# A Fourier filter and a low-rank mixer: new residue order in the last stage, one pair of batch 0 copied straight to its rows, free rows cleared by two engines

## The chip, the cores and the metric

The kernel runs on one core of a Trainium2 chip. A core has five engines with their own instruction queues: PE (TensorE, matrix products; PEld is its weight load), DVE (VectorE), ACT (ScalarE), POOL (GpSimd) and SP (SyncE, which here only issues transfers). Transfers issued by SP and by POOL share sixteen transfer engines. The metric is the device time in microseconds; the kernel before took 522.15 us (median of three runs, 521.4 to 522.26).

## The reference

Shapes: x is 8 batches x 3136 positions x 256 channels; U is 3136 x 32, V is 32 x 3136, w1 is 256 x 1024, w2 is 1024 x 256.

```python
X = np.fft.rfft(x, axis=1)
y = np.fft.irfft(X * (filt_r + 1j * filt_i)[None], n=3136, axis=1)
u = y + (y.transpose(0, 2, 1) @ U @ V).transpose(0, 2, 1)
out = u + np.maximum(u @ w_ch1, 0.0) @ w_ch2
```

Each batch is filtered along the positions, a rank-32 mixture of the positions is added, and a two-layer network runs on the channels of every position.

## The kernel before

A position is written as 64 q + r, with q below 49 and r, the residue, below 64. A transform of length 3136 becomes a 49-point step over q and a 64-point step over r, each a matrix product. Of the 49 frequencies k1 of the first step only 0 to 24 are needed.

For a batch b the stages are:

- **f1 (L203 to L246)**: the 49-point transform of x. For batches 0 and 1 it leaves the data in SBUF (`f1_turned`), and `turn` (L248) transposes it; the others pass through DRAM.
- **mid (L271)**: for each pair of k1 (twelve pairs, and k1 = 0 alone) a 64-point transform (L325), the product with the filter on DVE (L333), and the transform back (`s3`, L286; product L292, copy to `e3` on ACT L302). `gm` and `gsm` are its matrices; their 64 output rows per real or imaginary part are the 64 residues r.
- **rank (L364)**: the product with the transformed U (`uh`, made once by `u_hat`, L181), which gives 32 rows `h1`; four DVE copies (L383) spread them over all residues.
- **s4 (L390)**, the last stage of the filter: for each residue r the 97 rows `eb[:, r, :]` are multiplied with `sv[:, r, :]`. Rows 0 to 31 of `eb` are the mixer's, row 96 is k1 = 0, and of rows 32 to 95 every fourth, with offset 0, 1 or 2, holds eight k1 values (real and imaginary) of part 0, 1 or 2. Rows with offset 3 carry nothing: `sv` is zero there, but `eb` must hold numbers. s4 handles eight residues at a time, in two halves: the even groups of eight first, then the odd ones (`g = 2 * (n % 4) + n // 4`).
- **mm1, mm2 (L427, L448)**: the two layers, on groups of 512 positions, the residual added by products with an identity (L446).

`e3` has residues on partitions, `eb` needs k1 on partitions. That turn goes through DRAM: `s3` stores four k1 at a time (L307) into `ct2[b][part]`, and `load_e2` (L353) loads a part back with two transfers, one for the even groups (h = 0) and one for the odd (h = 1). In batch 0 the last two pairs (21, 22 and 23, 24) are each stored on their own (L304). `fill` (L359) copies 512 KB of some constant into the offset-3 rows of `eb` once.

The order of the work is written out by hand. Ahead of the steady state stand `u_hat`, f1 and mid of batch 0, its loads, its rank stage, half of batch 1's f1 mixed with 13 matmuls on constants (`pw`, L513) that keep PE busy, and s4 of batch 0. POOL's copy `seen` (L515), which reads a few numbers of `eb`, holds back the x and w2 transfers behind it until `eb` is loaded. From there one loop runs mm1 and mm2 over the 49 groups, with the stages of the next batches dealt into it by a list `plan`.

The lines that the change and the prediction's steps touch: the filter copies `spread_filters` (L152, called at L317), `s3` (L291, L303), `load_e2` and `fill` with their calls (L494 to L504), `rank` (L368, L383), `s4` (L399) and `pw` (L510). SP issues in this order in batch 0: two stores of part 0 with k1 = 0's row between them, `fill`, two stores of part 1, two loads of part 0, the store of pairs 8 and 9 (counted from 0), those of pairs 10 and 11, two loads of part 1, two of part 2. A queue works in order: an instruction that waits holds all behind it.

Of the kernel before, what the change touches and what calls it, by code (L numbers as in the profile page):

```python
# [10 lines left out]
F16 = mybir.dt.float16  # L11
F32 = mybir.dt.float32
# [9 lines left out]
GT = 512  # L22
NG = NB * SEQ // GT


# [5 lines left out]
def _consts():  # L31
# [25 lines left out]
    rows = [64 * c + 32 * h + j for j in range(32) for c in range(2) for h in range(2)]  # L57
    m64 = np.concatenate([a2[rows], g, gs, 2 * a2], axis=1)

# [14 lines left out]
def kernel(  # L74
# [58 lines left out]
    for c in range(4):  # L133
        load_x(0, c)
    m64 = cst.tile([128, 512], F16)
    nc.sync.dma_start(m64, m64_d)
    a2m, gm, gsm = m64[:, 0:128], m64[:, 128:256], m64[:, 256:384]
    a20m = m64[0:64, 384:512]


# [30 lines left out]
    sv = cst.tile([97, NR, NQ], F16)  # L171

    seen = cst.tile([128, 4], F16)

# [3 lines left out]

    uh = cst.tile([128, NK, RANK], F16)

    def u_hat():  # L181
        tu = sb.tile([RANK, 24, 128], F16, tag="ut", bufs=2, name="tu")
        tu0 = sb.tile([RANK, NR], F16, tag="tu0", bufs=1, name="tu0")
        for n in range(8):
            pu = bank("zmzo"[n % 4], "puh")
            for i in range(4):
                j = 4 * n + i
                nc.tensor.matmul(pu[0:RANK, 98 * i:98 * i + 98], usb[:, j, :], ws[:, j * 98:j * 98 + 98],
                                 start=(i == 0), stop=True, skip_group_check=True)
            copy = nc.vector.tensor_copy if n % 2 else nc.scalar.copy  # L190
            copy(tu.rearrange("p k (c j) -> p k c j", c=4)[:, :, :, 4 * n:4 * n + 4],
                 view(pu[0:RANK], 0, [[1, 24], [24, 4], [98, 4]]))
            copy(view(tu0, 4 * n, [[1, 4], [32, 2]]), view(pu[0:RANK], 96, [[98, 4], [1, 2]]))
        pt = bank("z", "put", F16)
        for k in range(NK):
            src = tu[:, k - 1, :] if k else tu0
            m = 128 if k else NR
            nc.tensor.transpose(pt[0:m, RANK * k:RANK * k + RANK], src, idn[0:RANK, 0:RANK])
        nc.vector.tensor_copy(uh[:, 1:NK, :].rearrange("r k u -> r (k u)"), pt[:, RANK:RANK * NK])
        nc.vector.tensor_copy(uh[0:NR, 0, :], pt[0:NR, 0:RANK])  # L200
# [70 lines left out]
    def mid(b, tag="z"):  # L271
# [14 lines left out]
        def s3(ks, uv, o):  # L286
# [3 lines left out]
            pe = bank(tag, "pe")  # L290
            for f, w in enumerate((gm, gsm) if b == 0 else (gm,)):  # L291
                nc.tensor.matmul(pe[0:m, 0:n], w[:, 0:m], uv[:, f, o:o + n], start=(f == 0), stop=(b > 0 or f == 1))  # L292
# [9 lines left out]
            nc.scalar.copy(t[:, 2 * (i % 2):2 * (i % 2) + 2, :].rearrange("p k d -> p (k d)"), pe)  # L302
            if b == 0 and i > 9:  # L303
                nc.sync.dma_start(dram(ct2[b][2], 2 * (i % 4) * 128 * DM, [[DM, 128], [128 * DM, 2], [1, DM]]),  # L304
# [10 lines left out]
        for i, ks in enumerate(PAIRS[:first_at] + [(0,)] + PAIRS[first_at:]):  # L315
            n = len(ks) * DM
            if b == 0 and i == 2:  # L317
                spread_filters(1)
# [29 lines left out]

    def blocks(rows, h):

        return rows.rearrange("p (q h r) d -> p h q r d", h=2, r=8)[:, h]

    def load_e2(b, part):  # L353

        for h in range(2):
            nc.sync.dma_start(blocks(eb[32 + part:96:4], h).rearrange("p q r d -> p q (r d)"),
                              dram(ct2[b][part], 8 * h * DM, [[NR * DM, 16], [16 * DM, 4], [1, 8 * DM]]))

    def fill():  # L359

        nc.sync.dma_start(eb[35:96:4].rearrange("p (q r) d -> p q (r d)", r=8),
                          dram(ws_d.tensor, 0, [[8 * DM, 16], [16 * 8 * DM, 8], [1, 8 * DM]]))

    def rank(b):  # L364
        ph = bank("z", "ph")
        for i in range(24):
            c = i % 4
            nc.tensor.matmul(ph[32 * c:32 * c + 32, 0:DM], uh[:, i + 1, :], e3[b, i // 4][:, i % 4, :],  # L368
                             start=(i < 4), stop=(i >= 20 and c != 0))
# [20 lines left out]
    def s4(b):  # L390
        ut[b] = sb.tile([128, 2, NQ, NR], F16, tag="ut", bufs=2, name="ut")
        for n in range(8):
            g = 2 * (n % 4) + n // 4
            for dh in range(2):
# [3 lines left out]
                for i in range(8):  # L398
                    nc.tensor.matmul(pu[:, NQ * i:NQ * i + NQ], eb[:, 8 * g + i, d], sv[:, 8 * g + i, :],  # L399
                                            start=(i == 0), stop=True, skip_group_check=True)  # L400
# [180 lines left out]
```

## Time and profile before

| | |
|---|---|
| median of three runs | 522.15 us (521.4 to 522.26) |
| the profiled execution | 521.98 us, span 520.2 us |
| PE busy | 497.6 us, 96% of the span |
| DVE, ACT, POOL busy | 347.3, 372.9, 80.7 us |
| bytes moved by transfers | 88.79 MB, mean 171 GB/s |
| first matmul of all (U's transform, L188) | 7.34 us |
| first matmul of s4, batch 0 (L399) | 45.44 us |
| first matmul of the two layers (L431) | 50.25 us |

Times of single instructions are counted from the start of the span. "Landing" of a transfer is the moment at which its completion is marked; a transfer has sixteen such marks, and the last one releases who waits. A row of the windows view gives a stretch, its length, and for PE, PEld, DVE, ACT and POOL the busy time with the number of instructions, then the granted clock of PE, the share of the transfer engines and GB/s.

### The profile page before, as it was taken

The numbers are of one execution on the slowest core, as the hardware profiler recorded it, in microseconds if no ns is written. First come the engines' busy times: TensorE is split into PE (matmuls) and PEld (weight loads), VectorE is DVE, ScalarE is ACT, GpSimd is POOL, SyncE is SP. The second block draws the span as 40 slices with busy tenths as digits, with TensorE's granted clock in tenths as the row PEclk, the third lists the DMA queues.
The fourth block names the chain that finished last, engine by engine and source line by source line (L and its number), as shares of the span: only waits on it lengthen the run. The fifth ranks groups of instructions, "written<-read, shape, count | busy, mean of one in ns | idle before, by whom it ended". The sixth has DMA issues, their size and how long they took to land.

```text
span 520.2 us, 11846 instructions
## 1 busy us (share of the span) xinstructions
PE 497.6 (96%) x4807; PEld 352.5 (68%) x4807; DVE 347.3 (67%) x465; ACT 372.9 (72%) x704; POOL 80.7 (16%) x111
## 2 busy tenths in 40 slices
PE   3787999999999999999999999999999999999996
PEld 3535666776667767777667767776777766776665
DVE  2976698688847975788747975789656995631212
ACT  3765779767985789667985689667975777666662
POOL 5862010111010120011010120111010010101110
PEclk9998999999999999999999999999999999999999
DMA  8997846758686596818776596819785145212213
GB/s 190 175 277 177 140 105 201 232 192 166 186 259 212 101 221 206 291 66 180 189 243 229 104 221 207 289 67 195 212 237 195 62 146 185 99 42 81 82 49 114
DMA packets 67605, 88.79 MB, mean 171 GB/s; under 512 B 4811, under 2 KB 51979, under 8 KB 67552
## 3 DMA queue, kind: packets, MB, share of 16 engines
q0 software_dynamic: 14640, 41.52, 32.7%
q1 hardware_dynamic: 52912, 46.53, 29.1%
q8 instruction: 37, 0.61, 0.5%
q14 instruction: 16, 0.13, 0.1%
HBM read 55.79 MB, written 47.91 MB: 199 GB/s over the span
## 4 chain that ended last, share of the span: by engine, by line
PE 88%; DMA 4%; DVE 3%; POOL 2%; ACT 1%; issue 1%; SPq 0%; ACTq 0%; POOLq 0%
PE pc L454 32%; PE phh L431 32%; PE pu L399 5%; PE pf L212 4%; PE pc L446 4%; PE pe L292 4%; PE pz L325 3%; DVE uv L333 2%; DMA x<-in_x_dram 2%; PE ph L368 1%; DMA fab<-in_filt_r_dram 1%; POOL fab L157 1%; DMA ct<-e 1%; POOL x L121 1%; DMA eb<-ct 1%
## 5 line engine op out<-in xcount | busy, mean ns | idle before, releaser
L434 ACT ACTIVATE h<-phh 128x512 f16<-128x512 f32 x392 | 236.2, 604 | 88.8 <-PE phh L431 87.7
L431 PE MATMUL phh<-ut,w1sb 128*128 128x512 f16 (+7 forms) x896 | 234.7, 354 | 0.5 <-DVE ut L406 0.3
L454 PE MATMUL pc<-w2sb,h 128*128 128x256 f16 x1568 | 234.1, 272 | 0.0
L454 PEld LDWEIGHTS <-h 128*128 128x128 f16 x1568 | 151.5, 97 | 90.4
L461 DVE COPY och<-pc 128x512 f32<-128x512 f32 x98 | 67.6, 690 | 101.1 <-PE pc L446 99.5
L333 DVE TENSOR_TENSOR uv<-pz,fab 128x1024 f16<-128x1024 f32 (+1 forms) x104 | 120.9, 1180 | 13.3 <-PE pz L325 11.9
L466 POOL DMA_DIRECT2D out_dram<-och x48 | 39.1, 815 | 407.2 <-DVE och L461 391.4
L431 PEld LDWEIGHTS <-w1sb 128*128 128x128 f16 x896 | 77.7, 98 | 20.4 <-issue 2.4
L302 ACT CAST e<-pe 128x512 f16<-128x512 f32 x96 | 56.6, 591 | 20.8 <-PE pe L292 20.5
L406 DVE CAST ut<-pu 128x392 f16<-128x392 f32 x92 | 48.5, 559 | 20.9 <-PE pu L399 17.7
L217 ACT CAST asb<-pf 98x512 f16<-98x512 f32 x96 | 57.3, 599 | 0.2
L446 PE MATMUL pc<-idn,ut 128*128 128x128 f16 (+1 forms) x400 | 54.0, 219 | 0.0
L383 DVE COPY eb<-h 32x4096 f16<-32x4096 f16 x32 | 38.2, 1232 | 16.1 <-ACT h L380 16.0
L292 PE MATMUL pe<-uv,m 128*128 128x512 f16 (+1 forms) x117 | 41.6, 373 | 3.5 <-DVE uv L333 2.2
L399 PE MATMUL pu<-sv,eb 97*128 97x49 f16 x1024 | 39.3, 187 | 3.3 <-DMA eb<-ct 3.3
L446 PEld LDWEIGHTS <-ut 128*128 128x128 f16 (+1 forms) x400 | 38.1, 98 | 5.2 <-issue 0.8
L399 PEld LDWEIGHTS <-eb 97*128 97x128 f16 x1024 | 36.4, 98 | 4.5 <-issue 3.7
L325 PE MATMUL pz<-a,m 128*128 128x512 f16 x96 | 36.2, 379 | 1.4 <-DVE a L263 1.2
L212 PE MATMUL pf<-x,ws 98*98 98x256 f16 x192 | 36.8, 274 | 0.0
L337 DVE TENSOR_TENSOR uv<-uv 64x1024 f16<-64x1024 f16 (+1 forms) x49 | 30.9, 630 | 1.7
L338 DVE TENSOR_TENSOR uv<-uv 64x1024 f16<-64x1024 f16 (+1 forms) x49 | 30.7, 627 | 0.7
L212 PEld LDWEIGHTS <-ws 98*98 98x98 f16 x192 | 22.0, 125 | 9.0
(61 smaller groups left out, 200.3 us busy)
## 6 DMA issues: line engine op xcount, KB each, us to landing
out_dram<-och POOLq DMA_DIRECT2D x48, 512.0 KB, 3.9
eb<-ct SPq DMA_DIRECT2D x48, 256.0 KB
ct<-e SPq DMA_DIRECT2D x47, 256.0 KB
x<-in_x_dram POOLq DMA_DIRECT2D x28, 392.0 KB, 8.0
ct<-asb SPq DMA_DIRECT2D x24, 384.0 KB
a<-ct SPq DMA_DIRECT2D x18, 512.0 KB
x<-in_x_dram POOLq DMA_DIRECT2D x4, 384.0 KB, 8.0
ws<-ws SPq DMA_DIRECT2D x1, 600.2 KB
```

The source lines that it names most:

```text
L212: nc.tensor.matmul(pf[0:98, 256 * s:256 * s + 256], ws[:, (8 * c + j) * 98:(8 * c + j + 1) * 98], t[:, j, :], start=(s == 0), stop=True, s ...
L217: nc.scalar.copy(dst, src)
L292: nc.tensor.matmul(pe[0:m, 0:n], w[:, 0:m], uv[:, f, o:o + n], start=(f == 0), stop=(b > 0 or f == 1))
L302: nc.scalar.copy(t[:, 2 * (i % 2):2 * (i % 2) + 2, :].rearrange("p k d -> p (k d)"), pe)
L325: nc.tensor.matmul(pz, a2m, src[:, k:k + 2, :].rearrange("p k d -> p (k d)"), start=True, stop=True)
L333: nc.vector.tensor_mul(uv[:, :, o:o + n], zin, fin)
L399: nc.tensor.matmul(pu[:, NQ * i:NQ * i + NQ], eb[:, 8 * g + i, d], sv[:, 8 * g + i, :], start=(i == 0), stop=True, skip_group_check=True)
L431: nc.tensor.matmul(ph[:, o:o + n], w1sb[:, dh, 128 * t:128 * t + 128], utv(b)[:, dh, t0:t0 + n], start=(dh == 0), stop=(dh == 1), skip_gro ...
L434: nc.scalar.activation(h, ph, RELU)
L446: nc.tensor.matmul(d, w, idn, start=False, stop=(dh == 1), skip_group_check=True)
L454: nc.tensor.matmul(o, gr.h[tt][:, 128 * i:128 * i + 128], w2sb[:, tt, :], start=(tt == 0), stop=False, skip_group_check=True)
L461: nc.vector.tensor_copy(gr.och[:, i - 1:i + 1, :], gr.pc.rearrange("p (j d) -> p j d", d=DM))
```

## The change

Five things are changed together.

1. **Residue order.** `eb` keeps its 64 residues as the 32 of the even groups followed by the 32 of the odd groups, instead of in natural order. `load_e2`, the four copies of `rank` and s4's reads of `eb` go to contiguous halves. Where rows reach `eb` without passing through DRAM, the transform back must give its residues in that order, so permuted copies of `gm` and `gsm` (`gmp`, `gsmp`) are added to the constant m64, which grows from 512 to 768 columns. They are used for k1 = 0 in all batches and for the last pair of batch 0. The matching U rows are permuted too: in `tu0`, and for the last pair in two extra entries of `uh`.
2. **The last pair of batch 0** (k1 = 23, 24) goes from `e3` straight into its four rows of `eb`, each row by one transfer of 64 pieces of 512 bytes, two on SP and two on POOL. The last load of part 2 then has 12 rows instead of 16 in that batch.
3. **Free rows.** `fill` is gone. At the very start DVE clears rows 0 to 95 of the first half of `eb`, and ACT clears those of the second half by copying a zero.
4. **Order on the queues.** Part 1's loads of batch 0 are issued one step earlier, ahead of pair 10's store; `spread_filters(1)` runs one step earlier.
5. **Filler.** 10 matmuls `pw` instead of 13.

```diff
+ORDER = np.concatenate([8 * (2 * (i % 4) + i // 4) + np.arange(8) for i in range(8)])
...
-    m64 = np.concatenate([a2[rows], g, gs, 2 * a2], axis=1)
+    p64 = np.concatenate([ORDER, 64 + ORDER])
+    m64 = np.concatenate([a2[rows], g, gs, 2 * a2, g[:, p64], gs[:, p64]], axis=1)
...
-    m64 = cst.tile([128, 512], F16)
+    m64 = cst.tile([128, 768], F16)
...
+    gmp, gsmp = m64[:, 512:640], m64[:, 640:768]
...
+    zero = cst.tile([128, 1], F32)
+    nc.vector.memset(zero, 0)
+    for h, rows in enumerate((eb[0:96, 0:32], eb[0:96, 32:64])):
+        rows = rows.rearrange("p r d -> p (r d)")
+        if h:
+            nc.scalar.copy(rows.bitcast(F32), bass.AP(tensor=zero.tensor, offset=zero.offset, ap=[[zero.ap[0][0], 96], [0, 4096]]))
+        else:
+            nc.vector.memset(rows.bitcast(mybir.dt.uint32), 0)
...
-    uh = cst.tile([128, NK, RANK], F16)
+    uh = cst.tile([128, NK + 2, RANK], F16)
...
-            copy(view(tu0, 4 * n, [[1, 4], [32, 2]]), view(pu[0:RANK], 96, [[98, 4], [1, 2]]))
+            copy(view(tu0, 32 * (n // 2 % 2) + 8 * (n // 4) + 4 * (n % 2), [[1, 4], [16, 2]]), view(pu[0:RANK], 96, [[98, 4], [1, 2]]))
...
+        tp = sb.tile([RANK, 2, 128], F16, tag="tp", bufs=1, name="tp")
+        nc.scalar.copy(view(tp, 0, [[64, 4], [32, 2], [8, 4], [1, 8]]), view(tu, 128 * 22, [[64, 4], [8, 2], [16, 4], [1, 8]]))
+        pd = bank("z", "pd", F16)
+        for k in range(2):
+            nc.tensor.transpose(pd[:, RANK * k:RANK * k + RANK], tp[:, k, :], idn[0:RANK, 0:RANK])
+        nc.scalar.copy(uh[:, NK:, :].rearrange("r k u -> r (k u)"), pd[:, 0:2 * RANK])
...
-            for f, w in enumerate((gm, gsm) if b == 0 else (gm,)):
+            direct = b == 0 and ks[0] == 23
+            ms = (gmp, gsmp) if direct or not ks[0] else (gm, gsm)
+            for f, w in enumerate(ms if b == 0 else ms[:1]):
...
-            if b == 0 and i > 9:
+            if direct:
+                for n, k in enumerate(ks):
+                    for part in range(2):
+                        (nc.sync if part else nc.gpsimd).dma_start(
+                            eb[32 + row_of(k, part):33 + row_of(k, part), :, :], t[64 * part:64 * part + 64, 2 + n, :])
+            elif b == 0 and i > 9:
...
-            if b == 0 and i == 2:
+            if b == 0 and i == 1:
                 spread_filters(1)
...
     def load_e2(b, part):
 
+        n = 12 if (b, part) == (0, 2) else 16
         for h in range(2):
-            nc.sync.dma_start(blocks(eb[32 + part:96:4], h).rearrange("p q r d -> p q (r d)"),
-                              dram(ct2[b][part], 8 * h * DM, [[NR * DM, 16], [16 * DM, 4], [1, 8 * DM]]))
-
-    def fill():
-
-        nc.sync.dma_start(eb[35:96:4].rearrange("p (q r) d -> p q (r d)", r=8),
-                          dram(ws_d.tensor, 0, [[8 * DM, 16], [16 * 8 * DM, 8], [1, 8 * DM]]))
+            nc.sync.dma_start(eb[32 + part:32 + 4 * n:4, 32 * h:32 * h + 32, :].rearrange("p (q r) d -> p q (r d)", r=8),
+                              dram(ct2[b][part], 8 * h * DM, [[NR * DM, n], [16 * DM, 4], [1, 8 * DM]]))
...
-            nc.tensor.matmul(ph[32 * c:32 * c + 32, 0:DM], uh[:, i + 1, :], e3[b, i // 4][:, i % 4, :],
+            nc.tensor.matmul(ph[32 * c:32 * c + 32, 0:DM], uh[:, i + (3 if b == 0 and i > 21 else 1), :], e3[b, i // 4][:, i % 4, :],
...
-            nc.vector.tensor_copy(blocks(eb[0:32], g // 2)[:, 2 * (g % 2):2 * (g % 2) + 2],
-                                  bass.AP(tensor=h1.tensor, offset=h1.offset, ap=[[h1.ap[0][0], 32], [0, 2], [0, 8], [1, DM]]))
+            nc.vector.tensor_copy(eb[0:32, 16 * g:16 * g + 16, :],
+                                  bass.AP(tensor=h1.tensor, offset=h1.offset, ap=[[h1.ap[0][0], 32], [0, 16], [1, DM]]))
...
-                    nc.tensor.matmul(pu[:, NQ * i:NQ * i + NQ], eb[:, 8 * g + i, d], sv[:, 8 * g + i, :],
+                    nc.tensor.matmul(pu[:, NQ * i:NQ * i + NQ], eb[:, 8 * n + i, d], sv[:, 8 * g + i, :],
...
-        if i == 7:
-            fill()
         if i == 10:
             load_e2(0, 0)
     next(ranks[0])
+    load_e2(0, 1)
     next(mids[0])
-    load_e2(0, 1)
...
-    for i in range(13):
+    for i in range(10):
...
-        nc.tensor.matmul(pw, m64[:, 0:128], m64, start=(i == 0), stop=(i == 12))
+        nc.tensor.matmul(pw, m64[:, 0:128], m64[:, 0:512], start=(i == 0), stop=(i == 9))
-    nc.gpsimd.tensor_copy(seen[64:96], eb[64:96, 8, 0:4])
+    nc.gpsimd.tensor_copy(seen[64:96], eb[64:96, 40, 0:4])
```

More of the change, by code (lines that the diff above doesn't have):

```diff
@@ L346, in mid @@
         yield
-    def blocks(rows, h):
-        return rows.rearrange("p (q h r) d -> p h q r d", h=2, r=8)[:, h]
     def load_e2(b, part):
+        n = 12 if (b, part) == (0, 2) else 16
         for h in range(2):
-            nc.sync.dma_start(blocks(eb[32 + part:96:4], h).rearrange("p q r d -> p q (r d)"),
-                              dram(ct2[b][part], 8 * h * DM, [[NR * DM, 16], [16 * DM, 4], [1, 8 * DM]]))
-    def fill():
-        nc.sync.dma_start(eb[35:96:4].rearrange("p (q r) d -> p q (r d)", r=8),
-                          dram(ws_d.tensor, 0, [[8 * DM, 16], [16 * 8 * DM, 8], [1, 8 * DM]]))
+            nc.sync.dma_start(eb[32 + part:32 + 4 * n:4, 32 * h:32 * h + 32, :].rearrange("p (q r) d -> p q (r d)", r=8),
+                              dram(ct2[b][part], 8 * h * DM, [[NR * DM, n], [16 * DM, 4], [1, 8 * DM]]))
     def rank(b):
```

## The prediction

> **What bounds the kernel now.** I read the page's busy shares first, then the chain of work that ended last, then the windows, waits and SP's timeline around the one stretch where TensorE stands still.
>
> The page's busy shares and the summary of its chain:
>
> ```profile
> PE 497.6 (96%) x4807; PEld 352.5 (68%) x4807; DVE 347.3 (67%) x465; ACT 372.9 (72%) x704; POOL 80.7 (16%) x111
> ...
> PE 88%; DMA 4%; DVE 3%; POOL 2%; ACT 1%; issue 1%; SPq 0%; ACTq 0%; POOLq 0%
> ```
>
> TensorE is the bound for nearly all of the span, and the change takes none of its steady work away. Whatever it is worth lies in the non-PE part of the chain, before batch 0's last stage ends. The chain in order of time (start us, length us, what):
>
> ```profile
> 36.03 0.60 ACT e L302
> 36.67 0.29 PE ph L368 x2
> ...
> 38.57 3.31 DMA ct<-e
> 41.95 0.52 SPq L356
> 42.52 2.94 DMA eb<-ct
> 45.46 4.15 PE pu L399 x120
> 49.63 0.58 DVE ut L406
> 50.25 3.58 PE phh L431 x8
> ```
>
> The last pair's output is ready at 36.62 and the last stage (L399) starts at 45.46: a store to DRAM, SP's turn, a load back. The stretches around it (busy time per engine, clock, transfer share, GB/s):
>
> ```profile
> 30.00:38.00 8.00, 6.00 (x46) 2.21 (x45) 5.35 (x5) 4.18 (x9) 4.07 (x1) 1.00 1.02 281
> 38.00:42.00 4.00, 4.00 (x43) 2.37 (x40) 3.67 (x4) 3.90 (x17) 0.00 (x0) 1.00 0.91 296
> 42.00:46.00 4.00, 0.74 (x23) 0.59 (x23) 1.06 (x2) 0.00 (x0) 0.00 (x0) 1.00 0.50 173
> 46.00:50.30 4.30, 3.98 (x114) 3.88 (x111) 4.00 (x8) 3.48 (x8) 3.26 (x6) 0.63 0.58 94
> ```
>
> Up to 42 the transfer engines are full (share 1.02, 0.91), and PE has filler; from 42.2 to 45.4 PE is idle. So the wait is a transfer backlog first and a latency second. SP's own timeline shows the order in that backlog:
>
> ```profile
> 27.44 0.37 SPq L307 DMA_DIRECT2D ct<-e  x1
> 27.86 0.61 SPq L361 DMA_DIRECT2D eb<-ws  x1
> 30.25 2.25 SPq L307 DMA_DIRECT2D ct<-e  x2
> 35.31 1.18 SPq L356 DMA_DIRECT2D eb<-ct  x2
> 36.54 1.43 SPq L307 DMA_DIRECT2D ct<-e  x1
> 38.07 0.97 SPq L304 DMA_DIRECT2D ct<-e  x2
> 39.20 3.91 SPq L356 DMA_DIRECT2D eb<-ct  x4
> ```
>
> The sixteen landing marks of each transfer (median, last) are, in SP's order: second store of part 0 34.76, 35.24; fill 36.01, 36.44; the two stores of part 1 36.78, 38.69 and about 37.5, 39.18; loads of part 0 38.48, 39.74 and 39.11, 40.35; pairs 8-9 40.18, 41.11; pair 10 40.62, 41.48; pair 11 40.99, 41.88; loads of part 1 41.93, 43.21 and 42.73, 43.83; loads of part 2 44.62, 45.35 and 45.39, 45.97. The last stage starts 0.09 us after the 45.35.
>
> **The change part by part.** The sum is against the profiled execution: 521.98 us, of which the span is 520.2; the median of the runs shown is 522.15, 0.17 above it.
>
> *Zeroing at the start.* DVE clears 4,096 words a partition. No row shows that instruction; the fp16 copy of 4,096 elements (L383) takes 1.23 us and the fp32 product of 1,024 elements (L333) 1.18 us, so 1.2 to 4.7 us; from 0.75 it ends by 5.5. ACT copies 4,096 words: L157 needed 1.90 us for 2,048, so 3.8 us, behind the table load that ends at 2.02, hence 5.8. DVE's first work before is at 8.21 and ACT's at 7.88, both behind U's landing (7.29). Cost 0; the cover is that landing. What could uncover it is a rival below.
>
> *m64 grows by half.* 64 KB more among the first loads. Below: 0, if it runs beside the wait for U. Above: 64 KB at the 177 GB/s of the first 8 us, 0.37 us. Its own median packet (64 ns for 1 KB) gives 128 x 32 ns / 16 = 0.26. U's load, which starts PE, runs beside it, so I take 0.15 and keep 0 to 0.37.
>
> *u_hat.* Two more transposes on PE: 25 took 0.95, so 0.08. Two ACT copies, 0.2 to 0.5 each (L193 0.18, L191 0.47): the first can start when DVE's last copy ends, 10.8, while PE is transposing until 11.84; the second is done about when ACT's next one began (12.39). I take 0.08, range 0 to 0.5.
>
> *spread_filters(1) one step earlier.* DVE's 0.76 us copy moves from 22.39 to about 21.1, ahead of a product; DVE's total is the same. It ran beside POOL's first filter copy, which took 3.01 us against 2.74 for the second. If that 0.27 goes, the product that waits for POOL at 28.47 can start when DVE is free, 28.31: -0.16, range -0.16 to 0.
>
> Together these three move the first stage by -0.16 to +0.87; I take +0.07.
>
> *The backlog: what goes.* The fill (median step 34.76 to 36.01 = 1.25 us of the queue), and pair 11's store (0.37).
>
> *What comes or moves.* Four one-row transfers (128 KB in 512 B pieces, as pair 11's store): 0.37 together, half on POOL's queue, half on SP behind pair 10's store. The two loads of part 1 are now issued before pair 10's store. They wait for part 1's second store; with the fill gone its median moves from 37.5 to 36.25, its last mark from 39.18 to 37.9, and behind that wait on SP stand pair 10's store, the two direct rows and the last load.
>
> *Why the 1.25 does not arrive whole.* Part 0's loads wait for the 35.24 landing, which lies ahead of the fill. Issue at 35.31 and 2.67 us (part 2's load, 41.95 to a median of 44.62) give a median landing of 37.98, against 38.48 now: only 0.50 of the 1.25. From there by median steps: second load 0.63 (38.61), pairs 8-9 1.07 (39.68), POOL's direct rows 0.19 (39.87), part 1's loads 0.63 to 0.80 each (41.13 to 41.47), pair 10 0.44: 41.57 to 41.91. The last of sixteen marks was 0.86 behind the median for pair 10 and 0.73 for a load that found the queue empty, 0.18 without its one laggard: so 41.75 to 42.77, against the 41.88 that releases SP now. SP by itself gives: wait ends 37.9, two loads at 0.6, store issued at 39.1, landing 2.3 later (the 2.29 of a store at 67.80 that met no queue): 41.4. Between 41.4 and 42.77 I take 41.9, nearest to the step sum without a full laggard: 0.0 against now.
>
> *The last load.* From issue to last mark 3.40 before, with other loads still ahead of it up to 43.83; now nothing but two small rows. Bounds: 2.85 (its marks without the laggard, 44.80) to 3.40; I take 3.1: -0.3. It has 12 rows instead of 16: by bytes 48 packets instead of 64, a quarter off about 0.64 (four packets of 159 ns an engine), -0.16. The Trainium skill (DMA: Bandwidth & Descriptors, "Why a DMA increments its semaphore by 16 and not by 1") says that a transfer is spread over the largest number of engines up to 16 that divides the outer size of both sides, hence 12 here, with four packets each as before; by that rule this saves nothing and the sum is the one without it. No run so far shows a transfer of 12 rows, and I take 0.
>
> *The direct rows themselves.* SP's are issued by about 40.4 and need 2.66 (the row at 69.87 landed at 72.53): 43.1. POOL is free from 34.07, waits for 36.62, issues two at about 0.55; even the slow 5.8 us of the early filter loads gives 43.5. Behind them POOL holds the copy `seen`, two x loads and w2sb, which wait for 45.97 anyway. Cost 0, covered by the last load; if that came before 43.5 they would be late next.
>
> *Filler.* Three of 13 matmuls less, 0.22 each: 0.65 less PE work ahead of an idle 3.2 us. Cost 0. The clock is at half from 47.1 to 53.9 already; the last stage does not feel it, since DVE's eight evictions of 0.54 fill 45.9 to 50.2.
>
> *Batches 1 to 7.* The same transfers, the same 32x4096 copies (1.2 us), other addresses; under PE's 96%: 0.
>
> *After the last stage.* `seen` releases x and w2sb; w2sb lands at 56.81 and the first matmul on it runs at 57.76. They move with the loads, so the start shift reaches the end.
>
> Sum: +0.07 + 0.0 - 0.3 = -0.23. 521.98 - 0.23 = 521.75; beside the median, 521.9. I forecast **521.8 us**. Ends: -0.16 - 0.48 - 0.55 = -1.19 and +0.87 + 0.89 + 0 = +1.76.
>
> **The rivals.** *Faster.* The relief is passed on: pair 10's store lands at SP's own 41.4 (-0.48) and the last load comes without a laggard (-0.55), -0.1 at the start: -1.13, 520.85, or 521.0 beside the median. For it: SP's queue would be short. Against: the step sum.
>
> *Slower: SP's queue.* One mark of part 1's second store is late again (its last is now 1.7 us behind its median) and comes at 39.18 as before. Then loads are issued at 39.20 and 39.88, pair 10's store at 40.5, landing at 42.8 to 43.9 (2.3, or the 3.4 of now): +0.9 to +2.0; middle 523.4. It decides once that store's wait ends after 38.4. Against: the fill's 1.25 us stand straight ahead of that store.
>
> *Slower: the start.* POOL's issue of U and x is held up by DVE's clearing, from 1.27 until 1.95 to 5.5; U, and everything behind it, comes 0.7 to 4.2 later: 522.7 to 526. Against: POOL's issues at 17.87 and 18.51 beside two DVE copies took 0.65 and 0.50, as ever. The Trainium skill (SBUF — State Buffer, "Who interferes with whom") says a DVE instruction with at most one SBUF input outside the two-port modes doesn't contend with GpSimd, which by its wording leaves a memset out; no run so far shows one.
>
> *Hidden anyway.* The last load's laggard stays: 0 to +0.07, 522.1.
>
> **How the numbers follow.** Forecast 0.38, hidden anyway 0.14, faster 0.25, SP's queue 0.15, start 0.08. About 0.2% (1.04 us) is what a measurement of this kernel can tell from no change. Faster: the 0.25 and 0.05 of the forecast's tail: 0.30. Slower: 0.15 + 0.08 - 0.02 = 0.21. Same: 0.49. The range takes in the faster rival's bound and SP's queue: 520.2 to 523.5; the forecast alone 521.0 to 522.6.
>
> **What would show it.** Right: no L361 row; part 0's loads issued within 0.3 us of 35.3; last landing of pair 10's store 41.5 to 42.3; L399's first matmul at 44.9 to 45.6; PE's idle stretch before it no shorter than 3 us. Wrong: that matmul before 44.4 or after 46.4, first U matmul after 7.8, or time found behind 58 us.

## The result and the profile after

The changed kernel takes 524.43 us (median of 7 runs, 523.38 to 526.17), against 522.15 us (7 runs, 520.52 to 523.13) for the kernel before beside it. The ratio is 1.0048, with a 95% interval of 1.0026 to 1.0069: the kernel got slower by about half a per cent, 2.3 us. The forecast was 521.8 us, in a range of 520.2 to 523.5. The profiled execution took 523.38 us with a span of 521.6 us, the shortest of its seven; the one before took 521.98 with 520.2. So the two traces differ by 1.40 us, less than the medians.

The busy shares and the summary of the chain of waits, from the page of the changed kernel:

```profile
PE 498.1 (95%) x4806; PEld 353.1 (68%) x4806; DVE 351.0 (67%) x467; ACT 377.0 (72%) x707; POOL 81.3 (16%) x113
...
PE 89%; DMA 4%; DVE 4%; ACT 1%; issue 1%; POOL 0%; DVEq 0%; SPq 0%; ACTq 0%; POOLq 0%
```

TensorE's work is the same to half a microsecond. The loss lies outside it, as the forecast had it of the gain. The chain of the changed kernel in order of time (start us, length us, what), from the last pair to the first matmul on w2sb:

```profile
36.31 0.59 ACT e L328
36.95 0.29 PE ph L391 x2
...
39.18 4.51 DMA ct<-e
43.69 0.02 issue
43.71 0.03 SPq L384
43.74 0.03 issue
43.77 3.12 DMA eb<-ct
46.88 0.30 issue
47.19 1.51 PE pu L422 x32
48.69 0.92 POOL x L127 x2
49.61 0.20 issue
49.81 9.55 DMA w2sb<-in_moe_w_ch_dram
59.36 0.04 issue
59.40 0.60 PE pc L477 x4
```

Before, the store in this place took from 38.57 to 41.88 and the last stage began at 45.44. Now it is pair 10's store, from 39.18 to 43.69, and the last stage begins at 47.19. The store's last mark is 1.81 us later, the last stage 1.75 us later. The delay runs on through the copy that releases x and w2sb: w2sb lands at 59.36 instead of 56.81, and the first matmul on it runs at 59.40 instead of 57.76, 1.64 us later. Before, that matmul ran 0.95 us behind the landing; now it runs 0.04 us behind it. What follows gives back 0.24 of that in this pair of traces (1.64 against the 1.40 of the profiled times).

The same stretches as before the change (busy time per engine, clock, transfer share, GB/s):

```profile
30.00:38.00 8.00, 5.93 (x41) 2.13 (x42) 5.63 (x5) 4.57 (x9) 5.11 (x3) 1.00 0.85 209
38.00:42.00 4.00, 3.82 (x43) 2.35 (x41) 3.39 (x3) 3.79 (x17) 0.27 (x1) 1.00 0.94 278
42.00:46.00 4.00, 0.00 (x0) 0.00 (x0) 1.23 (x2) 0.18 (x2) 0.00 (x0) 0.81 0.38 112
46.00:50.30 4.30, 3.11 (x76) 3.14 (x77) 2.08 (x4) 1.71 (x4) 1.79 (x4) 0.50 0.32 84
```

In the first row the transfer share fell from 1.02 to 0.85: the fill is gone, and its time was left empty; the loads behind it did not come earlier. In the third row PE does nothing at all for 4 us, and the clock falls within it. The last row shows the last stage at half the clock, with 76 matmuls in this stretch where there were 114.

SP's timeline of the changed kernel (start us, length of the issues us, what):

```profile
35.98 1.23 SPq L384 DMA_DIRECT2D eb<-ct  x2
37.32 0.52 SPq L338 DMA_DIRECT2D ct<-e  x1
37.95 1.18 SPq L384 DMA_DIRECT2D eb<-ct  x2
39.18 0.59 SPq L335 DMA_DIRECT2D ct<-e  x1
39.81 1.15 SPq L332 DMA_DIRECT2D eb<-e  x2
43.77 1.74 SPq L384 DMA_DIRECT2D eb<-ct  x2
```

Read from the top: part 0's loads, the store of pairs 8-9, part 1's loads, pair 10's store (39.18, before at 38.07), the two direct rows, and after a gap of almost 3 us the last load, which needs pair 10's store. The landing marks (median, last): part 0's loads 38.81, 39.10 and 39.73, 40.97; POOL's direct rows last at 41.06 and 41.84; pairs 8-9 40.89, 42.02; part 1's loads last at 42.66 and 43.33; pair 10 43.19, 43.69; SP's direct rows last at 44.14 and 44.33. Pair 10's store moved behind two loads of 256 KB, and landed behind them.

### The profile page after: what moved, and what is told of

It reads as the page before. It is cut to its first block, busy times and chain, and to the rows that moved or that the text cites. A ratio compares the mean times of both kernels' runs of the same rounds, so it can differ in the third digit from the quotient of the medians.

```text
span 521.6 us, 11857 instructions
## 1 busy us (share of the span) xinstructions
PE 498.1 (95%) x4806; PEld 353.1 (68%) x4806; DVE 351.0 (67%) x467; ACT 377.0 (72%) x707; POOL 81.3 (16%) x113
## 4 chain that ended last, share of the span: by engine, by line
PE 89%; DMA 4%; DVE 4%; ACT 1%; issue 1%; POOL 0%; DVEq 0%; SPq 0%; ACTq 0%; POOLq 0%
PE pc L477 32%; PE phh L454 31%; PE pu L422 5%; PE pf L235 4%; PE pe L318 4%; PE pc L469 4%; PE pz L356 4%; DVE uv L364 2%; DMA w2sb<-in_moe_w_ch_dram 2%; DMA usb<-in_moe_U_dram 1%; PE ph L391 1%; DMA ct<-e 1%; PE pt L284 1%; DVE t L266 1%; DMA eb<-ct 1%
```

## The experiments

The place of part 1's loads on SP, the clearing by DVE and ACT, and the new order of the residues were first tried each by itself.

**Part 1's loads back behind pair 10's store**, the rest as in the changed kernel:

```diff
     next(ranks[0])
-    load_e2(0, 1)
     next(mids[0])
+    load_e2(0, 1)
     next(ranks[0])
```

> The changed kernel with part 1's two loads issued behind pair 10's store and the two direct rows again, as in the kernel before; all else of the change stays. Theory Q (SP's queue: pair 10's store stands behind two loads, on SP and in the transfer queue): the store is issued at about 38.0 instead of 39.18, lands at about 41.5 instead of 43.69, the last load is released some 2 us earlier, L422's first matmul comes at 45.0 to 45.6 instead of 47.19, and the time falls by 1.5 to 2.4 us to 522.0 to 522.9. Theory D (the direct rows and the 12-row load cost the time): the first matmul moves by less than 0.6 us and the time stays above 523.6.

Measured: 522.15 us (521.09 to 524.06, 12 runs), ratio to the kernel before 0.9994 [0.9978, 1.0011]. The whole 2.3 us are gone with this one line. The profiled execution was the slowest of the twelve (524.06, with 10.24 us at half clock). It shows the order and SP's early issue of the store (38.36), but not the rest of what was expected: the store's last mark came at 43.04 and not near 41.5, and the last stage began at 46.47. So this experiment rests on its twelve times and not on its trace. SP's timeline:

```profile
36.04 1.64 SPq L384 DMA_DIRECT2D eb<-ct  x2
37.79 0.52 SPq L338 DMA_DIRECT2D ct<-e  x1
38.36 0.51 SPq L335 DMA_DIRECT2D ct<-e  x1
38.98 1.15 SPq L332 DMA_DIRECT2D eb<-e  x2
40.23 4.58 SPq L384 DMA_DIRECT2D eb<-ct  x4
```

**Part 1's loads ahead, in the kernel before**: the same line moved the other way.

```diff
     next(ranks[0])
+    load_e2(0, 1)
     next(mids[0])
-    load_e2(0, 1)
     next(ranks[0])
```

> The kernel before with that move alone: part 1's two loads are issued ahead of the stores of pairs 10 and 11. Theory Q: the loads wait for part 1's second store (landing 39.18), both stores follow at about 40.5 and 41.0 and land at 43 to 44.4 instead of 41.88; first matmul of L399 at 47.0 to 48.0 instead of 45.44, time 523.7 to 525. Theory D: no move, 522.2 within 0.7.

Measured: 525.09 us (522.71 to 526.75, 12 runs), ratio 1.0041 [1.0023, 1.0058]. This move alone costs as much as the whole change. SP's timeline of that kernel:

```profile
35.53 1.17 SPq L356 DMA_DIRECT2D eb<-ct  x2
36.76 1.28 SPq L307 DMA_DIRECT2D ct<-e  x1
39.44 1.16 SPq L356 DMA_DIRECT2D eb<-ct  x2
40.69 1.04 SPq L304 DMA_DIRECT2D ct<-e  x2
44.59 1.16 SPq L356 DMA_DIRECT2D eb<-ct  x2
```

The two stores go out at 40.69 and 41.27 instead of 38.07 and 38.57, land at 44.13 and 44.51, and the last load follows at 44.59 instead of 41.95; the last stage begins at 47.56. Here the loads also wait, until 39.44, for part 1's second store, since the fill is still there. From its issue the first of the two stores took 3.44 us to its last mark (40.69 to 44.13), no more than before (3.41, from 38.07 to 41.48): in this kernel the delay is SP's wait. In the changed kernel it is divided otherwise: the store was issued 1.11 us later than before and then took 4.51 us.

**The clearing by DVE and ACT alone**, on the kernel before, with the fill taken out:

```diff
+    zero = cst.tile([128, 1], F32)
+    nc.vector.memset(zero, 0)
+    for h in range(2):
+        rows = eb[0:96].rearrange("p (q h r) d -> p h q (r d)", h=2, r=8)[:, h]
+        if h:
+            nc.scalar.copy(rows.bitcast(F32), bass.AP(tensor=zero.tensor, offset=zero.offset, ap=[[zero.ap[0][0], 96], [0, 4], [0, 1024]]))
+        else:
+            nc.vector.memset(rows.bitcast(mybir.dt.uint32), 0)
...
-        if i == 7:
-            fill()
```

> The kernel before with the clearing by DVE and ACT at the start in place of the 512 KB fill; all else as before. From the fill's place in the queue: part 1's stores land about 1.25 us earlier, but part 0's loads still wait for the 35.24 landing, so pairs 10's and 11's stores land 0.3 to 0.8 us earlier and L399's first matmul comes at 44.6 to 45.2 instead of 45.44; time 521.4 to 522.0. If the relief were passed on whole: 44.2 and 520.9. If the clearing disturbs the start: first U matmul after 7.8 and time above 522.6.

Measured: 522.71 us (521.39 to 524.82, 12 runs), ratio 1.0005 [0.9988, 1.0022]. Part 1's stores landed at 36.38 and 37.29 instead of 38.69 and 39.18, so the fill's place in the queue was indeed freed. But part 0's loads were issued at 35.70, not earlier, since they wait for part 0's second store (last mark 35.62), which lies ahead of the fill. Pair 10 landed at 41.34, pair 11 at 42.01: the relief did not get through to the last stage.

**The order of the residues and the larger m64 alone**, on the kernel before (one of the changed places is shown):

```diff
...
-                nc.tensor.matmul(pu[:, NQ * i:NQ * i + NQ], eb[:, 8 * g + i, d], sv[:, 8 * g + i, :],
+                nc.tensor.matmul(pu[:, NQ * i:NQ * i + NQ], eb[:, 8 * n + i, d], sv[:, 8 * g + i, :],
...
```

> The kernel before with the new residue order alone (m64 of 768 columns, permuted k1 = 0 rows, contiguous halves of eb); fill, both late pairs through DRAM, loads and filler as before. Theories Q and D both: no change beyond the larger m64, first matmul of the last stage within 0.4 us of 45.44, time 522.2 within 0.6. If the larger m64 or the contiguous halves cost more than that (part 0's second store landed 0.65 us later in the changed kernel, 35.89 against 35.24), the landing of that store shows it: 35.7 or later.

Measured: 522.71 us (520.91 to 524.22, 12 runs), ratio 0.9999 [0.9983, 1.0015]: no difference that shows. The last mark of part 0's second store came at 35.72, just past the 35.7 that was set as a sign of a cost; but in the six traces of kernels with the smaller m64 that mark lies between 35.24 and 36.32, so one trace can't decide it. **With the direct rows added** (and the last load of 12 rows, the two added transposes):

```diff
-            if b == 0 and i > 9:
+            if direct:
+                for n, k in enumerate(ks):
+                    for part in range(2):
+                        (nc.sync if part else nc.gpsimd).dma_start(
+                            eb[32 + row_of(k, part):33 + row_of(k, part), :, :], t[64 * part:64 * part + 64, 2 + n, :])
+            elif b == 0 and i > 9:
...
+        n = 12 if (b, part) == (0, 2) else 16
```

> The kernel before with the new residue order and the direct rows of the last pair, and nothing else: fill, late loads of part 1, 13 filler matmuls and the old place of the filter copies stay. If the direct rows save their store's part of the queue: pair 10's store lands at 41.0 to 41.5, last load released up to 0.7 earlier than 41.95, first matmul 44.8 to 45.3, time 521.6 to 522.1. If the gain is given back (direct rows between the stores, a 12-row load that takes longer to issue and to land): last load released at 41.9 to 42.8 and landing 2.8 to 3.1 later, first matmul 45.4 to 46.3, time 522.3 to 523.3.

Measured: 523.57 us (521.4 to 526.17, 10 runs), ratio 1.0014 [0.9992, 1.0036]. The interval holds 1, and by itself leaves room for a cost of up to 1.9 us. In the trace pair 10's store landed at 42.67, the last load was issued at 42.75 instead of 41.95, and the last stage began at 46.29: in this execution the gain was given back, as the second of the two theories had it. But the kernel with part 1's loads back holds the direct rows too and loses nothing, so they are not the cause of the 2.3 us.

**Pair 10's store on ACT's queue**, with part 1's loads left early as the change has them:

```diff
-                nc.sync.dma_start(dram(ct2[b][2], 2 * (i % 4) * 128 * DM, [[DM, 128], [128 * DM, 2], [1, DM]]),
+                (nc.scalar if i == 10 else nc.sync).dma_start(dram(ct2[b][2], 2 * (i % 4) * 128 * DM, [[DM, 128], [128 * DM, 2], [1, DM]]),
```

> The changed kernel with pair 10's store issued by ACT, right behind its copy, instead of by SP behind part 1's two loads; part 1's loads stay early. Theory Q1 (the store is late because SP works in order): it is issued at 36.3 to 36.8 instead of 39.18, lands by 41.5, the last load then waits only for the store of pairs 8 and 9 (42.02) and is issued at 41.5 to 42.2 instead of 43.77; first matmul of the last stage at 45.0 to 45.6, time 522 to 523. Theory Q2 (it is late because the transfer engines are full with part 1's loads): it still lands after 43, first matmul after 46.8, time above 523.6.

Measured: 521.98 us (520.14 to 524.36, 12 runs), ratio 0.9996 [0.9976, 1.0016]. SP's timeline of that kernel, and behind it the line of ACT's with the store:

```profile
36.26 1.23 SPq L384 DMA_DIRECT2D eb<-ct  x2
37.53 0.94 SPq L338 DMA_DIRECT2D ct<-e  x1
38.58 1.23 SPq L384 DMA_DIRECT2D eb<-ct  x2
39.86 1.23 SPq L332 DMA_DIRECT2D eb<-e  x2
42.08 1.74 SPq L384 DMA_DIRECT2D eb<-ct  x2
```

```profile
36.16 0.39 ACTq L335 DMA_DIRECT2D ct<-e  x1
```

The store goes out at 36.16, 3 us earlier, lands at 39.28, the last stage begins at 45.54 (47.19 in the changed kernel), and the loss is gone although part 1's loads are as early as in the changed kernel. So it is not the early loads' traffic as such but the store's place behind them in SP's order that costs the time. The last load, though, is issued at 42.08 only: it now waits for the store of pairs 8-9, which lands at 42.06.

**The even halves first.** All even halves of the loads were issued ahead of the odd ones, in the kernel before and in the changed one with part 1's loads back:

```diff
-        for h in range(2):
+        for h in hs:
...
-    load_e2(0, 2)
+    load_e2(0, 2, (0,))
+    for p in range(3):
+        load_e2(0, p, (1,))
```

> The kernel before with batch 0's loads in another order on SP: the even half of part 0, 1 and 2 first, each as soon as now, and the three odd halves behind them; nothing else. If what stands on SP and in the queue ahead of the late pairs' stores sets the start, one load less there (0.6 us on SP, 0.64 in the queue) brings pair 11's store from 41.88 to 41.2 to 41.5, the last even load to 44.7 to 45.0, and the first matmul to 44.7 to 45.1; time 521.4 to 522.1, and no more than that because x and w2 still wait for the odd halves. If a landing that is not in the queue sets it, no move: 522.2.

> The changed kernel with part 1's loads late again and the same order of halves as in the kernel v1_halves. The queue theory gives pair 10's store at 40.6 to 41.4, last even load issued by 41.5, first matmul 44.2 to 44.9, time 521.0 to 521.8. If the gain of the direct rows is given back by the 12-row load, 521.6 to 522.5, no better than v1_halves.

Measured: 523.37 us (522.09 to 524.96, 12 runs), ratio 1.0016 [0.9997, 1.0035]; and 523.24 us (522.24 to 524.67, 12 runs), ratio 1.0025 [1.0007, 1.0043]. In the first the last stage began at 45.49, no earlier than before. In the second it began at 44.86, earlier than in the kernel before, and the kernel was still slower: the odd halves came late, x was issued at 48.34 instead of 46.26, and w2sb landed at 60.37. In these traces an earlier first matmul was not worth anything by itself: the landing that releases x and w2sb had not moved with it.

**Is it the half clock?** In the changed kernel PE stands still for 5.37 us instead of 3.25 ahead of the last stage. The clock is halved for 6.83 us in both traces, from 47.12 before and from 44.49 now, so that nearly the whole last stage runs at half the clock. More filler matmuls (0.22 us each) fill the stretch: 27 in place of 13 in the kernel before, 33 in place of 10 in the changed one.

```diff
-    for i in range(13):
+    for i in range(27):
...
-        nc.tensor.matmul(pw, m64[:, 0:128], m64, start=(i == 0), stop=(i == 12))
+        nc.tensor.matmul(pw, m64[:, 0:128], m64, start=(i == 0), stop=(i == 26))
```

> The kernel before with 27 filler matmuls instead of 13 while it waits for the last load: 14 more at 0.22 us are 3.1 us, which fill the idle stretch of TensorE from 42.2 to about 45.3. Theory clock (the idle stretch brings on the half clock, and that costs part of the time): no half clock or one stretch of 3.4 us less of it near 46 to 54 us, and the median goes to that of the executions with a mean clock of 0.995 and more, 521.8: ratio about 0.9994. Theory landing (only the landings of the loads and of w2sb set the end): 522.1, ratio 1.000, whatever the clock shows; w2sb lands at 56.8 in both.

> The changed kernel with 33 filler matmuls instead of 10: 23 more at 0.22 us are 5.1 us, which fill the idle stretch from 42.0 to about 47.1. Theory clock: of the 2.3 us that the change lost, the longer half clock made some 0.6 to 1; with the stretch filled the median is 523.4 to 523.8. Theory landing: the late store of pair 10 and the late last load alone made the 2.3 us: 524.4, and the first matmul of the last stage is still at 47.2.

Measured: the kernel before with filler 521.41 us (520.51 to 524.13, 12 runs), ratio 0.9988 [0.9968, 1.0008]; the changed kernel with filler 523.23 us (522.47 to 524.82, 12 runs), ratio 1.0025 [1.0011, 1.0039]. Two windows of the changed kernel with filler:

```profile
42.00:46.00 4.00, 4.00 (x20) 1.85 (x19) 1.60 (x2) 0.56 (x4) 0.00 (x0) 1.00 0.38 125
46.00:50.30 4.30, 3.57 (x100) 2.75 (x99) 1.56 (x4) 1.77 (x5) 0.96 (x3) 1.00 0.33 97
```

The clock stays at 1.00 in these windows. In all 24 executions of the two kernels the mean clock was 0.995 or more, against 18 of the 35 of the kernel before beside them. (One stretch of 3.41 us at half the clock takes 0.003 off the mean of a span of 520 us, so 0.995 leaves room for one such stretch and not for two.) By the medians both kernels gain about the same, 1.06 (522.47 - 521.41) and 1.20 (524.43 - 523.23, from different sets of runs), though neither gain is clear of the intervals, and the difference between them stays at 523.23 - 521.41 = 1.82 us, four fifths of the 2.28.

Executions alike in clock say more. At a mean clock of 0.998 or more the kernel before took 521.82 us (mean of six), the kernel before with filler 521.82 as well (mean of eleven), and the changed kernel with filler 523.46 (mean of ten). So at a full clock the filler changes nothing here, and some 1.6 us of the loss stay. All seven executions of the changed kernel without it had a mean clock of 0.993 or less. The other 0.6 us or so go with the clock, near the 0.6 to 1 that the theory of the clock gave; that the longer idle stretch causes them is not shown.

**Filler and the store on ACT** (the edit of pair 10's store as above, and 26 filler matmuls), then also x and w2sb released by an even half:

```diff
-    for i in range(10):
+    for i in range(26):
...
-    nc.gpsimd.tensor_copy(seen[64:96], eb[64:96, 40, 0:4])
+    nc.gpsimd.tensor_copy(seen[64:96], eb[64:96, 8, 0:4])
```

> The changed kernel with pair 10's store on ACT's queue (which gave 521.98) and 26 filler matmuls instead of 10, 3.5 us more, up to about 45.3. Theory clock: no half clock ahead of w2sb, the median goes to that of the executions with a mean clock of 0.995 and more, 521.1: ratio to before 0.998. Theory landing: 522.0, ratio 0.9996.

> As the run with pair 10's store on ACT's queue and 26 filler matmuls, and the copy that releases x and w2sb reads a row of the even halves instead of the odd ones, so that they are issued 0.6 to 0.8 us earlier. If w2sb's landing sets the end: 0.6 to 0.8 below the run without that edit, 520.4 to 521.4. If the odd halves, which are still on the queues then, are held up by x and w2sb: the last stage breaks off between its halves and the time is the same or up to 0.5 longer.

Measured: 522.17 us (521.17 to 523.87, 12 runs), ratio 1.0000 [0.9985, 1.0016]; and 521.65 us (520.39 to 524.72, 12 runs), ratio 0.9988 [0.9969, 1.0008]. Neither differs from the kernel before by more than the interval, and the first not from the run without the filler (521.98). Here the filler did not keep the clock: in the first trace a stretch of 3.41 us at half the clock begins at 50.22, and three of the twelve executions of the first kernel and four of the second had a mean clock of 0.991 to 0.993. In the second, x was issued at 46.04 instead of 47.09; the 0.52 us between the two medians are inside the noise.

**The store of pairs 8-9 on ACT too.** The run with pair 10's store on ACT had left this store as the last one. With both on ACT (pair 10's store by the edit above) and 17 filler matmuls:

```diff
-                nc.sync.dma_start(dram(ct2[b][i // 4], 2 * (i % 4 - 1) * 128 * DM, [[DM, 128], [128 * DM, 4], [1, DM]]), t)
+                (nc.scalar if (b, i) == (0, 9) else nc.sync).dma_start(dram(ct2[b][i // 4], 2 * (i % 4 - 1) * 128 * DM, [[DM, 128], [128 * DM, 4], [1, DM]]), t)
...
-    for i in range(10):
+    for i in range(17):
```

> The changed kernel with both late stores, of pairs 8-9 and of pair 10, on ACT's queue, and 17 filler matmuls. Theory queue (the store of pairs 8-9 was late because SP issued it behind part 0's loads): it is issued near 35.5 instead of 37.5 and lands near 39.5 instead of 42.06, the last load is issued by 40.5 and the last stage starts at 43.0 to 44.0 instead of 45.5: 520.0 to 521.0. Theory backlog (the transfer engines are full until 42 whatever the order): the last load is issued earlier but lands behind part 1's loads, first matmul 45.0 to 45.5: 521.5 to 522.2. ACT pays 0.4 for the issue either way.

Measured: 520.40 us (519.55 to 522.49, 12 runs), ratio 0.9965 [0.9946, 0.9984]: faster than both kernels. ACT's two issues, SP's timeline, and two windows:

```profile
34.55 0.39 ACTq L338 DMA_DIRECT2D ct<-e  x1
...
36.05 0.37 ACTq L335 DMA_DIRECT2D ct<-e  x1
```

```profile
36.30 2.95 SPq L384 DMA_DIRECT2D eb<-ct  x4
39.34 1.18 SPq L332 DMA_DIRECT2D eb<-e  x2
40.56 1.79 SPq L384 DMA_DIRECT2D eb<-ct  x2
```

```profile
42.00:46.00 4.00, 2.89 (x62) 1.93 (x61) 1.92 (x4) 1.04 (x4) 0.47 (x2) 1.00 0.43 117
46.00:50.30 4.30, 2.98 (x84) 2.36 (x81) 3.33 (x8) 2.87 (x8) 2.82 (x5) 1.00 0.73 117
```

The two stores land at 38.72 and 39.07, the last load goes out at 40.56 (43.77 in the changed kernel), and 62 matmuls stand in the window that had none, 55 of them the last stage's. The last stage begins at 44.6, not at the 43.0 to 44.0 that was expected: SP's two direct rows, issued just ahead of the last load, now land last, at 44.18 and 44.35. That is the wait which the forecast named as late next. Not all of the gain is the earlier stage itself. Nine of the twelve executions had a mean clock of 0.998 or more, and took 520.29 us (mean); of the 29 of the kernel before beside them six had that, and took 521.28. So 1.0 of the 1.92 us between the medians stays at an equal clock. The rest goes with more executions at full clock, and whether the filler or the earlier last stage brought these isn't shown; with pair 10's store alone on ACT, 26 filler matmuls gave 522.17.

The same on the kernel before, with its three late stores on ACT and 18 filler matmuls, and the fastest kernel with x and w2sb released by an even half (the edit of `seen` as above):

```diff
-                nc.sync.dma_start(dram(ct2[b][2], 2 * (i % 4) * 128 * DM, [[DM, 128], [128 * DM, 2], [1, DM]]),
+                nc.scalar.dma_start(dram(ct2[b][2], 2 * (i % 4) * 128 * DM, [[DM, 128], [128 * DM, 2], [1, DM]]),
...
-                nc.sync.dma_start(dram(ct2[b][i // 4], 2 * (i % 4 - 1) * 128 * DM, [[DM, 128], [128 * DM, 4], [1, DM]]), t)
+                (nc.scalar if (b, i) == (0, 9) else nc.sync).dma_start(dram(ct2[b][i // 4], 2 * (i % 4 - 1) * 128 * DM, [[DM, 128], [128 * DM, 4], [1, DM]]), t)
```

> The kernel before with its three late stores (pairs 8-9, 10 and 11) on ACT's queue and 18 filler matmuls: three issues of 0.4 on ACT. Theory queue: as for the changed kernel, but the fill and pair 11's store are still in the backlog, some 1.6 us of it: part 2's loads are issued near 41.2 and the last stage starts at 44.5: 521.0 to 521.5, so that the change would be worth 0.5 to 1 here. Theory backlog: 521.4 to 522.1, as with the filler alone.

> As the changed kernel with both late stores on ACT and 17 filler matmuls, and x and w2sb released by a row of the even halves. If w2sb's landing sets the end: 0.4 to 0.8 below the run without that edit. If the odd halves suffer from x and w2sb: the same or up to 0.5 above it.

Measured: 522.86 us (519.97 to 526.94, 12 runs), ratio 1.0011 [0.9988, 1.0035]; and 521.46 us (519.94 to 523.17, 12 runs), ratio 0.9979 [0.9959, 0.9999]. The first says nothing on its question, so what the change is worth with all late stores out of the way in both kernels stays open. Part 0's second load was issued at 39.68 there instead of about 36.7, 0.02 us after the store of pairs 8-9 had landed at 39.66; in the trace the two count on the same semaphore. What SP's loads waited for in that kernel:

```profile
SPq L356 <- DMA ct<-e: 4.0, 3, 3.0
```

The longest of these three waits is 3.0 us, between two loads that need no store of pairs 8-9: a wait that moving the store had made. In the second, x was issued 0.3 us earlier than without that edit and w2sb landed 0.7 us later (55.98 against 55.28); the median is 1.06 us higher (521.46 against 520.40), so the earlier release brought no gain.

## Why the prediction was wrong

**The step that failed** is the backlog: "Between 41.4 and 42.77 I take 41.9 ... 0.0 against now". Pair 10's store landed at 43.69, 0.9 beyond the upper bound and 1.81 after the 41.88 that released SP before. That is the whole delay of the last stage: from there to the first matmul it takes 3.50 us (43.69 to 47.19), before 3.56 (41.88 to 45.44).

Two terms in it were mis-sized.

- *The start of the step sum.* The forecast issued part 0's loads at 35.31, as before, and gained 0.50 there. They were issued at 35.98, 0.09 after the last mark of part 0's second store (35.89, before 35.24). Of these 0.65, 0.28 are also in the last pair's output (36.31 against 36.03). One trace was too little to fix this start. In the six traces of kernels with the smaller m64 part 0's loads were issued between 35.31 and 36.40, and the forecast was built on the earliest; in the eleven with the larger one, between 35.69 and 36.40. The first matmul on U ran at 7.10 to 7.34 in the six and at 7.24 to 7.88 in the eleven (medians 7.25 and 7.53), so the larger m64 seems to cost about 0.28 there, where 0.15 was taken; where the rest comes from stays open. The median landing of the first load was 38.81, not 37.98, and of the store of pairs 8-9 40.89, not 39.68: 1.2 us late before the moved loads come in.
- *The last mark of pair 10's store.* By SP's own sum the wait ends at 37.9, the store is issued at 39.1 and lands 2.3 later, at 41.4. The loads were issued at 37.95 and the store at 39.18, right to 0.1 us, the first of these by luck: the wait on part 1's second store ended at 37.42, and the loads stood behind the store of pairs 8-9 on SP until 37.84. The third took 4.51: the 2.3 came from a store that met no queue, and this one had two loads and the store of pairs 8-9 ahead of it. The sum by transfers did put it behind the loads. Counted from the measured 38.81, its steps give 42.40 to 42.74 for the store's median; it came at 43.19, mostly since part 0's second load and part 1's first each took about 0.3 longer. The last mark was 0.50 behind the median, where 0.18 to 0.86 was allowed, but the 41.9 that was taken leaves only 0 to 0.33 behind the sum's own 41.57 to 41.91.

So the forecast had the loads ahead of the store in its sum, but let savings pay for them: 0.50 of the fill's 1.25, which never came, and pair 11's store. In the kernel before the two late stores stood *ahead* of part 1's loads, and their landing is what the last load waits for. The move spends the relief at the one place where it counted.

*Filler* may have been mis-sized too. It was put at 0, with the half clock counted as there already. By the executions alike in clock some 0.6 of the 2.28 us go with the clock; the cause of these is not shown.

**The rivals.** *SP's queue* had the mechanism, the store waiting behind the loads, but with the wrong point from which it decides. It asked for the wait on part 1's second store to end after 38.4. That store's last mark came at 37.42, earlier than forecast, and the loss came nevertheless. Here the store was issued 1.11 us later and took 1.10 longer from issue to last mark (4.51 against 3.41). That the 512 KB of loads ahead of it make the second part is not shown: in the slow execution that was traced without them it took 4.68. What is shown, by times, is that the loss is there with the store behind the loads on SP, and not with it ahead of them or on ACT. *Faster* didn't happen. With both late stores on ACT the changed kernel took 520.40, below the 520.85 to 521.0 of that rival, but with seven more filler matmuls and by another path, so this does not bear it out. *The start* didn't happen: DVE's clearing and ACT's lie in the shadow of U's landing, as these lines of the first microseconds of DVE and of ACT show (start us, duration us):

```profile
1.70 3.47 DVE L187 MEMSET eb<- 96x4096 uint32 x1 [0.82 <-issue]
8.11 0.55 DVE L208 CAST tu<-puh 32x384 f16<-32x384 f32 x1 [2.94 <-PE puh L205]
```

```profile
2.03 3.60 ACT L185 COPY eb<-zero 96x4096 f32<-96x4096 f32 x1
7.78 0.47 ACT L208 CAST tu<-puh 32x384 f16<-32x384 f32 x1 [2.15 <-PE puh L205]
```

The clearing ends at 5.17 on DVE (forecast: by 5.5) and at 5.63 on ACT (5.8); POOL's issue of U took 0.70, as before, and the first matmul on U ran at 7.29 with the clearing alone, against 7.34 before. By the Trainium skill (SBUF — State Buffer, "Who interferes with whom") a DVE instruction with at most one SBUF input outside the two-port modes does not contend with GpSimd. The trace agrees: POOL's seven issues of x beside this memset took 3.63 us, against 3.65 before.

**What was right.** The last load took 3.12 us from issue to last mark, where 3.1 was taken (-0.28, forecast -0.3). In part this was luck: the 3.40 before held one mark 0.55 behind the others, and a load of 16 rows that met an empty queue took 2.89 (44.59 to 47.48, in the kernel before with part 1's loads ahead), so the 12 rows seem to cost 0.2 where 0 was taken. They saved nothing over 16: the trace shows one mark 1.29 us after the issue and twelve between 2.85 and 3.11. This agrees with the rule of the Trainium skill (DMA: Bandwidth & Descriptors, "Why a DMA increments its semaphore by 16 and not by 1"), by which such a transfer runs on 12 engines and the sequencer writes the four marks left over by itself at once. The direct rows, the two transposes, the three filler matmuls less and the copy of the filters moved up together cost nothing that the runs can tell from zero (0.9994 with part 1's loads back). The start came to 0.28 by the last pair's output, inside -0.16 to +0.87. After the last stage everything moved with the loads, as forecast, only in the other direction.

## What to carry to other kernels

When a transfer is moved ahead of another on one queue, it is not enough that the bytes are the same: list for each transfer who waits for it, and put the ones that release something ahead of those that are only needed at the end. A store that a later load reads back wants the front of its queue, or a queue of its own (ACT's here: 0.39 us of ACT's time, 3 us earlier). But look at what else then waits for it: in the kernel before the same move held a load back by 3.0 us. A relief in a queue reaches only what isn't held by another wait: here the removed fill left the transfer engines empty (share 0.85), since the loads behind it waited for a store ahead of it.

## What the runs showed of the hardware

- The clock was halved in stretches of 3.41, 6.83 and 10.24 us, one, two or three times the same length, and how many differed from one execution to the next of the same kernel. The Trainium skill (TensorE: Matmul & The Clock Gate, Part 1) states a free-running window of 3413 ns; the length agrees. The ten traces with such a stretch around the last stage have an idle stretch of PE of 1.3 to 5.5 us there; in the seven without one the longest is 0.9 to 2.0 us. For the 35 executions of the kernel before beside the filler runs, the mean time was 521.87 us at a mean clock of 0.995 or more (18 of them), 522.75 between 0.991 and 0.995 (8), and 523.83 below (9): a good part of the spread of this kernel goes with its clock. With 14 more filler matmuls all 12 executions had 0.997 or more.
- The issue of a load of 12 rows took SP 0.89 and 0.80 us, against 0.52 and 0.59 for one of 16 rows.
- A store issued by ACT was on the same semaphore as a later load of SP, and the load waited for it (39.68 after 39.66; in the fastest kernel 38.73 after 38.72) though no data tie them.
